# The last stores of an attention-and-feed-forward kernel, dealt anew to two DMA queues

## The chip, the cores and the metric

The kernel runs on one core of one Trainium2 chip. The metric is the device time of one execution in microseconds, as the median of several runs. All times below are microseconds, unless they are marked ns.

## What is computed

The first half is routing attention: queries and keys get a cluster by their nearest centroid, and a query sees only keys of its own cluster. The second half is a feed-forward block on the result. For this change only the end of the second half matters:

```python
scores = np.where(mask, scale * np.matmul(q, k.transpose(0, 1, 3, 2)), -1e9)
attn = softmax(scores)                      # rows
x = np.matmul(attn, v)                      # 4 batches, bridged to (3072, 512)
h = x @ w_in                                # (3072, 2048)
g = h * (1.0 / (1.0 + np.exp(-1.702 * h)))
out = g @ w_out                             # (3072, 512), float32
```

The output is 4 batches of 768 rows of 512 floats.

## The kernel before

`fast` does the whole work; `general` follows under a condition that these inputs don't meet, so every engine jumps over its code to the end of the program (line 34). After the attention, the feed-forward half runs batch by batch (`for b in range(B)`, B = 4). Each batch first makes the hidden values G with `first7`, then the output with seven calls of `second49`, one for each product in `ORDER = (1, 2, 3, 6, 5, 7, 4)` of a Strassen-like scheme. The output of a batch is held transposed in four quarters, Y[11], Y[12], Y[21] and Y[22]; each is 128 partitions by 2 (index m) by 384 (rows of the output). The quarters come complete in the order 11, 12, 22, 21.

`store(b, n, m, q, queues)` (line 940) brings quarter n, or a part of it, to the output. First VectorE transposes it in 32x32 blocks into another tile, one instruction (line 951) for each m. Then four DMAs (line 955), one for each group of 32 partitions, write it. `queues[r % len(queues)]` deals these four to the queues that are named: with `nc.sync` alone all go out on SyncE's queue (SPq in the profile), with `(nc.sync, nc.scalar)` they go out alternately on SyncE's and ScalarE's (ACTq). `q` selects halves of the rows, QT = 192 rows each. A whole quarter goes in DMAs of 32x12x64 floats (96 KB), half of its rows with both m in 32x6x64 (48 KB), half of its rows with one m in 32x6x32 (24 KB).

In the last batch the stores are placed in the last two calls of `second49` through `extra(at)`, which draws steps from generators. In the last call (k = 6, product 4) `tail()` is drawn. Its first step, at `extra(0)`, stores all of Y[22]. Its second step, at `extra(2)`, comes when all of Y[21] is complete except for the rows 0 to 191 of m = 1: these still lack the last product, which is added in line 928 (`add(c[:, 1, 0:QT], x, c[:, 1, 0:QT])`). After the loop over k, the last `store` brings these.

The order of instructions on each engine is the order in which they are recorded. Each DMA raises one of eight completion semaphores when it has landed, and it waits until the DMA that had this semaphore before has landed. The two queues share the eight semaphores. The built program shows which semaphore each DMA has: the third and fourth DMA of Y[22], on SPq, have numbers 4 and 5 and wait for the first and second DMA that ACTq issues for Y[21], which have the same numbers. The wait of a DMA for its data or its semaphore holds up everything behind it on the same queue.

Of the kernel before, what the change touches and what calls it, by code (L numbers as in the profile page):

```python
# [38 lines left out]
def fast(  # L39
# [26 lines left out]
    nc = tc.nc  # L66
# [4 lines left out]
    P = 128  # L71
# [12 lines left out]
    SQ = 32  # L84
# [520 lines left out]
    def sums_w(i):  # L605

        if i >= B * FB:
            return
        f = i % FB
        S = wq.tile([P, 3, 2, P], FP32, name="W")  # L610
        w_of[i] = {1: S[:, 0], 2: S[:, 1], 3: A_in(1, 0, f), 4: S[:, 2]}
        S = w_of[i]
        A11, A12, A22 = A_in(0, 0, f), A_in(0, 1, f), A_in(1, 1, f)
        if i < FB:
            sums(nc.gpsimd, ((S[3], A11, "-", S[3]),))
        sums(nc.gpsimd, ((S[2], A22, "-", S[3]), (S[1], S[2], "+", A11),
                         (S[4], A12, "-", S[2])))
# [122 lines left out]
    def sums_z(engine, f):  # L740
        sums(engine, ((Sz(3, f), Bz(0, 0, f), "-", Bz(0, 1, f)),
                      (Sz(2, f), Bz(1, 1, f), "-", Sz(3, f)),
                      (Sz(1, f), Sz(2, f), "+", Bz(0, 0, f)),
                      (Sz(4, f), Bz(1, 0, f), "-", Sz(2, f))))
# [16 lines left out]
    def turn_w(i):  # L761
        a = W_of(i)
        sums(nc.vector, ((a(0, 1), a(0, 0), "-", a(0, 1)),))

    def keep_w(k, o):

        a = W_of(ORDER[k])
        s2, s1, s4 = o
        for i, (o, x, op, z) in enumerate((
                (s2, a(1, 1), "-", a(0, 1)), (s1, s2, "+", a(0, 0)),  # L770
                (s4, a(1, 0), "-", s2))):
            sums(nc.gpsimd, ((o, x, op, z),))
            nc.sync.dma_start(out=kept_w[k, i], in_=o)

    def spare_y():
        return [Y[n].rearrange("p a t -> p (a t)")[:, 0:FQ * P].rearrange(
            "p (f n) -> p f n", n=P) for n in (12, 21, 22)]
# [3 lines left out]
    def load_sums(k, made=False):  # L781
        W[k] = ws.tile([P, 3, FQ, P], FP32, name="Wz")
        if made:
            keep_w(k, [W[k][:, i] for i in range(3)])
            return
        for i in range(3):
            nc.sync.dma_start(out=W[k][:, i], in_=kept_w[k, i])
# [50 lines left out]
    def first7(b, f, X, T):  # L838

        S = w_of.pop(b * FB + f)  # L840

        def product(a, x):
            ps = ps_b.tile([P, 512], FP32, name="b")
            for c in range(2):
                nc.tensor.matmul(out=ps[:, 0:HALF], lhsT=a[:, c], rhs=x(c),  # L845
                                 start=(c == 0), stop=(c == 1))
            return ps[:, 0:HALF]

        def finish(g):
            nc.scalar.activation(out=g, in_=g, func=AF.Gelu_apprx_sigmoid,  # L850
                                 scale=2.0)

        g1, g2 = G[:, f], G[:, f + FB]
        p = product(A_in(0, 0, f), lambda c: X[0, 0, c])
        nc.scalar.copy(g1[:, 0], p)
        p = product(S[2], lambda c: T[2, c])
        add(g2[:, 1], p, g1[:, 0])
        p = product(S[1], lambda c: T[1, c])
        add(g1[:, 1], p, g2[:, 1])
        p = product(S[3], lambda c: T[3, c])  # L860
        add(g2[:, 0], p, g2[:, 1])
        add(g2[:, 1], p, g1[:, 1])
        p = product(S[4], lambda c: X[1, 1, c])
        add(g1[:, 1], p, g1[:, 1])
        finish(g2[:, 1])
        p = product(A_in(1, 1, f), lambda c: T[4, c])
        add(g2[:, 0], p, g2[:, 0])
        finish(g1[:, 1])
        p = product(A_in(0, 1, f), lambda c: X[1, 0, c])
        add(g1[:, 0], p, g1[:, 0])  # L870
        finish(g2[:, 0])
        finish(g1[:, 0])

    def after7(f):

        sums(nc.vector, ((G[:, f, 1], G[:, f + FB, 1], "-", G[:, f, 1]),))
        if f >= FQ:
            for _ in sums_t(0, slice(f - FQ, f - FQ + 1)):
                pass
# [57 lines left out]
                    5: ((Y[12], y, "+", Y[12]), (Y[22], y, "+", Y[21])),  # L937
                    7: ((Y[22], y, "+", Y[22]), (Y[21], y, "+", Y[21]))}[i])

    def store(b, n, m=slice(0, 2), q=slice(0, 2), queues=(nc.sync,)):  # L940

        h, t = divmod(n, 10)
        h, t = h - 1, t - 1
        o = {11: T_of[4], 12: E[0], 22: E[1], 21: E[2]} if b < B - 1 else {
            11: T_of[4], 12: T_of[4], 22: T_of[2], 21: T_of[3]}
        o = o[n].rearrange("p a t -> p (a t)").rearrange(
            "p (j m i) -> p j m i", m=2, i=SQ)
        at, to = q.start * QT, q.stop * QT
        o = o[:, at // SQ:to // SQ]
        for one in range(m.start, m.stop):  # L950
            nc.vector.transpose(out=o[:, :, one], in_=Y[n][:, one, at:to])
        rows = out[b * S + t * HALF + at:b * S + t * HALF + to]
        for r in range(P // SQ):
            col = r * P + (2 * h + m.start) * SQ
            queues[r % len(queues)].dma_start(
                out=rows[:, col:col + (m.stop - m.start) * SQ].rearrange(
                    "(j t) i -> t j i", t=SQ),
                in_=o[r * SQ:(r + 1) * SQ, :, m].rearrange(
                    "t j m i -> t j (m i)"))
# [20 lines left out]
    def do(steps, n):  # L980
        for _ in range(n):
            next(steps, None)
# [3 lines left out]
    for b in range(B):  # L986
        for f in range(FB):
            first7(b, f, *XT)
            sums_w(b * FB + f + 2)
            if f:  # L990
                after7(f - 1)
            do(pend, 1)
            if b == 0 and f < 3:
                for n in range(3 * f, min(3 * f + 3, FB)):
                    sums_z((nc.gpsimd, nc.vector, nc.vector)[n % 3], n)
            if b == 0 and f in (3, 4):
                for i in ORDER[0:4] if f == 3 else ORDER[4:]:
                    turn_w(i)
            if b == 0 and f >= 3:
                for k in {3: (0,), 4: (1, 2), 5: (3,), 6: (4,), 7: ()}[f]:  # L1000
                    keep_w(k, spare_y())
                if 5 <= f < 7:
                    load_sums(f - 5)
        after7(FB - 1)
        if b < B - 1:
            for h in range(2):
                for hp in range(HP):
                    x = xT_of[b + 1, h, hp] = xp.tile([P, HALF], FP32,
                                                      name="x")
                    nc.sync.dma_start(out=x, in_=kept[b, h, hp])  # L1010
            made = sums_x(b + 1)
        else:
            made = iter(())

        def stores(b, *todo, **how):
            for n in todo:
                store(b, n, **how)
                yield

        both = dict(queues=(nc.sync, nc.scalar))  # L1020

        def tail():
            store(b, 22)
            yield
            store(b, 21, slice(0, 1), slice(0, 1), **both)
            store(b, 21, q=slice(1, 2), **both)
            yield

        def chain(*todo):
            for steps in todo:  # L1030
                yield from steps

        def sums_of_x():
            for XT[:] in made:
                yield

        x_steps = sums_of_x()
        final = b == B - 1

        for k in range(7):  # L1040
            nxt = sums_t(k + 1) if k < 6 else iter(())
            more = {1: sums_G(6), 2: sums_G(5), 3: sums_G(4),
                    4: stores(b, 11), 5: stores(b, 12) if final else x_steps,
                    6: tail() if final else x_steps}.get(k, iter(()))
            if b == B - 1 and k < 2:
                test(k)
            if (b, k) == (B - 1, 6):
                is_bad = nc.values_load(bad[0:1, 0:1], min_val=0, max_val=1)

            def extra(at):  # L1050
                do(nxt, (2, 1, 1)[at])
                do(more, ((1, 0, 1) if final else (0, 4, 4))[at] if k == 6
                   else (0, 0, 4)[at] if k == 2 else (0, 2, 2)[at])

            second49(k, extra, final)
            if k < 5:
                load_sums(k + 2, b == 0 and k > 2)
            elif b < B - 1:
                load_sums(k - 5)
        pend = () if final else stores(b, 12, 22, 21)  # L1060
        if final:
            store(b, 21, slice(1, 2), slice(0, 1), **both)
    return is_bad
@with_exitstack
def general(
# [436 lines left out]
```

## Time and profile before

| | us |
|---|---|
| median of 3 runs | 911.01 |
| lowest and highest | 910.65, 911.41 |
| the profiled execution, whole | 910.43 |
| span in its profile | 908.5 |
| TensorE busy | 888.4 |
| VectorE busy | 728.6 |
| GpSimd busy | 492.1 |
| ScalarE busy | 363.3 |

The profiled execution is 1.93 longer than its span: this part lies outside the recorded instructions. Positions in the profile, such as 897.36, are counted from the start of the span. A row of the timeline has start, length, engine, line, operation, output and input, and a count of instructions. A "q" after an engine (SPq, ACTq, DVEq, PEldq) marks its sequencer: issues of DMAs, waits and branches. The start of a DMA's row is the start of its issue, not of its transfer, and its length is that of the issue. TENSOR_TENSOR and STREAM_TRANSPOSE on DVE are VectorE's sums and transposes.

### The profile page before, as it was taken

The numbers are of one execution on the slowest core, as the hardware profiler recorded it, in microseconds if no ns is written. First come the engines' busy times: TensorE is split into PE (matmuls) and PEld (weight loads), VectorE is DVE, ScalarE is ACT, GpSimd is POOL, SyncE is SP. The second block draws the span as 40 slices with busy tenths as digits, with TensorE's granted clock in tenths as the row PEclk, the third lists the DMA queues.
The fourth block names the chain that finished last, engine by engine and source line by source line (L and its number), as shares of the span: only waits on it lengthen the run. The fifth ranks groups of instructions, "written<-read, shape, count | busy, mean of one in ns | idle before, by whom it ended". The sixth has DMA issues, their size and how long they took to land.

```text
span 908.5 us, 17741 instructions
## 1 busy us (share of the span) xinstructions
PE 888.4 (98%) x6712; PEld 577.7 (64%) x6712; DVE 728.6 (80%) x1170; ACT 363.3 (40%) x816; POOL 492.1 (54%) x469
## 2 busy tenths in 40 slices
PE   8999999999999999999999999999999999999994
PEld 3344444444444445557996557997557997557994
DVE  4999999998899997998998556797556797557894
ACT  3777767777676773322111222112222112222110
POOL 5899989998999998693274221243221243220220
PEclk9999999999999999999999999999999999999998
DMA  9465556666665210036213202322202322200323
GB/s 176 117 131 107 102 119 129 146 136 132 132 132 122 85 43 18 0 117 232 70 53 109 48 1 70 103 74 90 48 1 70 105 70 93 47 1 1 105 75 69
DMA packets 178397, 78.97 MB, mean 87 GB/s; under 512 B 155272, under 2 KB 161536, under 8 KB 178304
## 3 DMA queue, kind: packets, MB, share of 16 engines
q1 hardware_dynamic: 176912, 77.53, 35.4%
q8 instruction: 55, 0.90, 0.5%
q10 hardware_dynamic: 1392, 0.23, 0.2%
q14 instruction: 38, 0.31, 0.1%
HBM read 61.03 MB, written 16.70 MB: 86 GB/s over the span
## 4 chain that ended last, share of the span: by engine, by line
PE 81%; DVE 9%; DMA 3%; issue 2%; SPq 2%; ACT 2%; POOL 0%; DVEq 0%; ACTq 0%
PE b L845 32%; PE b L895 23%; PE s L467 11%; PE o L532 9%; PE m L549 3%; PE s L490 2%; DVE G L593 2%; DMA raw<-in_moe_w_out_dram 2%; DVE E L593 1%; ACT A L498 1%; SPq L418 1%; DVE Tx L593 1%; PE m L343 1%; DMA line<-row 1%; DVE x L570 1%
## 5 line engine op out<-in xcount | busy, mean ns | idle before, releaser
L516 POOL TENSOR_TENSOR sum<-sum,A 128x384 f32<-128x384 f32 x252 | 264.0, 1082 | 35.8 <-ACT A L498 22.6
L836 DVE TENSOR_TENSOR G<-b,G 128x384 f32<-128x384 f32 x224 | 123.0, 556 | 99.2 <-PE b L845 89.4
L498 ACT ACTIVATE A<-s 128x768 f32<-128x768 f32 x192 | 144.7, 803 | 93.9 <-PE s L490 73.8
L593 POOL TENSOR_TENSOR Y<-y,Y 128x768 f32<-128x768 f32 x28 | 67.4, 2422 | 175.0 <-DVE y L836 151.0
L467 PE MATMUL s<-T,T 64*64 64x384 f32 x1536 | 144.5, 491 | 2.7 <-ACT A L498 0.9
L850 ACT ACTIVATE G<-G 128x384 f32<-128x384 f32 x128 | 66.3, 523 | 198.9 <-DVE G L836 197.6
L532 PE MATMUL o<-A,inv 64*64 64x384 f32 x1536 | 141.3, 483 | 0.0
L593 POOL TENSOR_TENSOR W<-w_in 128x256 f32<-128x256 f32 x32 | 23.6, 736 | 164.2 <-PE b L845 163.8
L593 DVE TENSOR_TENSOR G<-G 128x768 f32<-128x768 f32 (+1 forms) x92 | 104.1, 1156 | 0.0
L467 PEld LDWEIGHTS s<-T,T 64*64 64x64 f32 x1536 | 52.0, 132 | 79.1 <-ACT A L498 52.0
L845 PE MATMUL b<-Tx,w_in 128*128 128x384 f32 x256 | 93.0, 486 | 0.0
L845 PE MATMUL b<-x,W 128*128 128x384 f32 x256 | 93.0, 486 | 0.0
L845 PE MATMUL b<-x,w_in 128*128 128x384 f32 x256 | 88.6, 486 | 0.0
L532 PEld LDWEIGHTS o<-A,inv 64*64 64x64 f32 x1536 | 58.7, 133 | 38.2 <-issue 33.3
L845 PEld LDWEIGHTS b<-x,W 128*128 128x128 f32 x256 | 48.6, 190 | 33.9
L845 PEld LDWEIGHTS b<-Tx,w_in 128*128 128x128 f32 x256 | 48.6, 190 | 33.9
L845 PEld LDWEIGHTS b<-x,w_in 128*128 128x128 f32 x256 | 48.5, 190 | 33.5 <-issue 0.6
L895 PE MATMUL b<-G,w_out 128*128 128x192 f32 x320 | 55.9, 326 | 0.0
L895 PEld LDWEIGHTS b<-G,w_out 128*128 128x128 f32 x320 | 52.7, 190 | 1.1
L895 PE MATMUL b<-E,Wz 128*128 128x192 f32 x288 | 51.5, 328 | 1.4 <-DVE E L593 1.4
L895 PEld LDWEIGHTS b<-E,Wz 128*128 128x128 f32 x288 | 47.1, 190 | 3.4 <-POOL Wz L593 1.3
L845 PE MATMUL b<-Tx,W 128*128 128x384 f32 x128 | 46.6, 487 | 1.5 <-DVE Tx L593 1.5
(169 smaller groups left out, 1357.5 us busy)
## 6 DMA issues: line engine op xcount, KB each, us to landing
Wz<-kept_w SPq DMA_DIRECT2D x78, 256.0 KB
raw<-in_moe_w_in_dram SPq DMA_DIRECT2D x16, 512.0 KB
raw<-in_moe_w_out_dram SPq DMA_DIRECT2D x16, 512.0 KB
inv<-in_v_dram SPq DMA_DIRECT2D x16, 384.0 KB
in<-in_q_dram SPq DMA_DIRECT2D x60, 96.0 KB
in<-in_k_dram SPq DMA_DIRECT2D x60, 96.0 KB
kept<-x SPq DMA_DIRECT2D x24, 192.0 KB
x<-kept SPq DMA_DIRECT2D x24, 192.0 KB
```

The costliest lines, as they stand in the source:

```text
L343: nc.tensor.matmul(out=ps[r:r + SQ, w * NJ * SQ:(w + 1) * NJ * SQ] .rearrange("p (j t) -> p j t", t=SQ), lhsT=cT[:, p % HP].rearrange("p a ...
L467: nc.tensor.matmul(out=ps[c:c + D, a, 0:HALF], lhsT=T[p, 1][rows, kt * P + c:kt * P + c + D], rhs=T[p, 0][rows, h * HALF:(h + 1) * HALF], ...
L490: nc.tensor.matmul(out=s_of[u][c:c + D, a, :], lhsT=rows_of[1, p % 2][rows, kt * P + c:kt * P + c + D], rhs=rows_of[0, p % 2][rows, h * HA ...
L498: nc.scalar.activation(out=A_of[u], in_=s_of.pop(u), func=AF.Exp, scale=SCALE)
L516: nc.gpsimd.tensor_tensor(out=sum_of[g][:, a], in0=(A_of[u - 1] if kt == 1 else sum_of[g])[:, a], in1=A_of[u][:, a], op=ALU.add)
L532: nc.tensor.matmul(out=o_of[g][a * D:(a + 1) * D, r, 0:HALF], lhsT=v_in[p][rows, a, kt, :], rhs=A[rows, a, :], start=(kt == 0), stop=(kt = ...
L549: nc.tensor.matmul(out=ps[a * D:(a + 1) * D, 0:HALF], lhsT=twos, rhs=sm[:, a, :], start=(i == 0), stop=(i == len(parts) - 1))
L593: engine.tensor_tensor(out=o, in0=a, in1=b, op=(ALU.add if op == "+" else ALU.subtract))
L836: nc.vector.tensor_tensor(out=o, in0=p, in1=a, op=ALU.add)
L845: nc.tensor.matmul(out=ps[:, 0:HALF], lhsT=a[:, c], rhs=x(c), start=(c == 0), stop=(c == 1))
L850: nc.scalar.activation(out=g, in_=g, func=AF.Gelu_apprx_sigmoid, scale=2.0)
L895: nc.tensor.matmul(out=ps, lhsT=A[n][:, f], rhs=M[n][:, f], start=start and f == 0, stop=(f == FQ - 1), skip_group_check=True)
```

## The change

Four parts, all in the last batch:

1. `store` gets a parameter `turned`, which says which m are transposed in this call, apart from `m`, which says which go out. With `queues=()` it only transposes.
2. In the second step of `tail()`, the rows 192 to 383 of Y[21], both m, are transposed and stored first, in four DMAs of 48 KB, all on SyncE's queue. Before, they were stored on both queues.
3. After that, m = 0 of the rows 0 to 191 is only transposed. Before, it was transposed first and stored in four DMAs of 24 KB on both queues.
4. After the loop, m = 1 of the rows 0 to 191 is transposed, and both m go out in four DMAs of 48 KB on both queues. Before, m = 1 alone went out in four DMAs of 24 KB.

Y[22] is stored by the same call as before.

```diff
-    def store(b, n, m=slice(0, 2), q=slice(0, 2), queues=(nc.sync,)):
+    def store(b, n, m=slice(0, 2), q=slice(0, 2), queues=(nc.sync,),
+              turned=slice(0, 2)):
...
-        for one in range(m.start, m.stop):
+        for one in range(turned.start, turned.stop):
             nc.vector.transpose(out=o[:, :, one], in_=Y[n][:, one, at:to])
         rows = out[b * S + t * HALF + at:b * S + t * HALF + to]
-        for r in range(P // SQ):
+        for r in range(P // SQ if queues else 0):
...
-        both = dict(queues=(nc.sync, nc.scalar))
-
         def tail():
             store(b, 22)
             yield
-            store(b, 21, slice(0, 1), slice(0, 1), **both)
-            store(b, 21, q=slice(1, 2), **both)
+            store(b, 21, q=slice(1, 2))
+            store(b, 21, q=slice(0, 1), queues=(), turned=slice(0, 1))
             yield
...
         if final:
-            store(b, 21, slice(1, 2), slice(0, 1), **both)
+            store(b, 21, q=slice(0, 1), turned=slice(1, 2),
+                  queues=(nc.sync, nc.scalar))
```

## The prediction

> **What bounds the kernel now.** I read the page first, then the chain of waits near the end, then the timeline of the two queues that issue stores, then SyncE's own waits, the branch at line 34, and the DMA traffic.
>
> ```profile
> span 908.5 us, 17741 instructions
> ...
> q8 instruction: 55, 0.90, 0.5%
> ...
> q14 instruction: 38, 0.31, 0.1%
> ...
> PE 81%; DVE 9%; DMA 3%; issue 2%; SPq 2%; ACT 2%; POOL 0%; DVEq 0%; ACTq 0%
> ```
>
> TensorE bounds the kernel as a whole (81% of the chain), but the change doesn't touch its work. The chain of waits from 895 on shows where arithmetic ends:
>
> ```profile
> 894.86 0.18 PE b L895
> ...
> 897.36 0.38 DVE Tx L951
> ```
>
> The last transpose ends at 897.74, 10.8 before the end of the span. These 10.8 are stores and the way out, and only they can change. The issues in them, each from a narrow window of the timeline:
>
> ```profile
> 887.94 1.91 SPq L955 DMA_DIRECT2D out_dram<-Tx  x4
> 891.99 0.83 SPq L955 DMA_DIRECT2D out_dram<-Tx  x2
> 898.14 1.85 SPq L955 DMA_DIRECT2D out_dram<-Tx  x2
> 896.59 0.85 ACTq L955 DMA_DIRECT2D out_dram<-Tx  x2
> 897.54 0.40 ACTq L955 DMA_DIRECT2D out_dram<-Tx  x1
> 898.52 1.46 ACTq L955 DMA_DIRECT2D out_dram<-Tx  x1
> 900.82 0.97 SPq L955 DMA_DIRECT2D out_dram<-Tx  x2
> 901.89 1.92 SPq L955 DMA_DIRECT2D out_dram<-Tx  x4
> ```
>
> Y[22] is ready at 891.96, and two of its four stores are issued at 891.99. The other two go out only at 898.14. They wait for completion semaphores 4 and 5, which ACTq's first two stores of Y[21] hold; these are issued at 896.59 and land just before 898.14. Its fourth issue takes 1.39 of the 1.85. Then SyncE waits 0.8 more for ACTq's third store (semaphore 6), until 900.8, and issues six stores of Y[21] in 0.97 + 1.92 with small gaps, until 903.82. SyncE's waits say the same:
>
> ```profile
> SPq L955 <- DMA out_dram<-Tx: 6.1, 2, 5.3
> SPq L34 <- SPq L34: 2.7, 1, 2.7
> ```
>
> The 5.3 is 892.82 to 898.14. The 2.7 is the branch at line 34:
>
> ```profile
> L34 SPq EVENT_SEMAPHORE  x8: 17/17/17, 906.6 to 907.2; - x8
> ...
> L34 ACTq COMPARE_BRANCH  x1: 54/54/54, 900.5 to 900.5; - x1
> L34 ACTq EVENT_SEMAPHORE  x1: 17/17/17, 903.3 to 903.3; - x1
> L34 SPq COMPARE_BRANCH  x1: 45/45/45, 903.9 to 903.9; - x1
> ```
>
> From branch to next instruction VectorE takes 2.8 (897.44 to 900.27), ScalarE 2.8 and SyncE 2.7: a fixed price. SyncE's last store landed at 905.34 by the trace's semaphore records, 1.3 before SyncE went on at 906.6. So the end is set by **SyncE's last issue**: 903.82, plus 2.8 to 906.6, plus 1.9 of closing steps to 908.5.
>
> **What the Trainium skill says.** Its page "DMA: Bandwidth & Descriptors", section "Why a DMA increments its semaphore by 16 and not by 1", says that each of up to 16 DMA engines adds one when its share has landed, so that only the full count means landed. The trace agrees, and shows stragglers: ACTq's third store had 15 of its 16 counts by 899.78, and the last one at 900.76. The page "Runtime: NRT & Kernel Launch", section "Instruction fetch mechanics", says that code comes by DMA in blocks of 16 KiB and that a taken branch must fetch its target. The trace has such fetches on the queues q8 and q14:
>
> ```profile
> DMA packets 595, 0.17 MB, mean 120 GB/s; under 512 B 593, under 2 KB 593, under 8 KB 593
> ...
> q8 instruction: 1, 0.02, 5.9%
> q14 instruction: 1, 0.01, 2.4%
> ```
>
> That is the window 898.2 to 899.6. The one packet on q8 has 16 KB and lasts from 898.26 to 899.57; the packet records show no store's packet from the engine that it sits on until 899.56. This makes the straggler. It comes 0.6 after TensorE's instruction at line 34 (897.67), so it belongs to TensorE, which the change leaves alone. The DMA page's section "Issuing engines are not separate DMA queues" says that both queues end up on the same 16 engines; the straggler, which a fetch imposes on a store of ACTq and through it on SPq, agrees.
>
> **The change, part by part.**
>
> *Y[22] (same call, other semaphores).* In the changed program its four stores have semaphores 6, 7, 0 and 1. Their last users are loads of line 787 and stores of Y[12], all landed by 890.6. So all four issue at 891.99, in the 1.91 that Y[12]'s four took: until 893.9. The 5.3 wait and the 1.85 of issue at 898.14 go. SyncE is free long before the next data.
>
> *Rows 192 to 383 of Y[21], SPq alone.* Their two transposes come first now, ready at 896.83 (two of the three in the 896.19 row, 0.89). The four 48 KB stores have semaphores 2, 3, 4 and 5. Numbers 2 and 3 are free: two issues from 896.84 to about 897.7. Numbers 4 and 5 are what ACTq's two stores use, and in the program's order those come first. So **the wait is not removed but moved**: the third store of this half waits until ACTq's first store has landed. Behind it on SPq stand one more store of this half, both last stores of SPq, the branch and the end.
>
> *VectorE.* Four transposes and one sum as before, in another order: nothing. The last transpose still ends at 897.74, since TensorE's part was ready at 896.33 already. If the order cost something it would be one transpose, 0.34.
>
> *Number of DMAs.* Before, twelve for Y[21], six on each queue; now eight, six of them on SPq and two on ACTq. SPq has six as before, but two are issued early, so four stand behind the wait instead of six.
>
> *ACTq.* It now waits for the last transpose (897.75), then issues its first store until 898.1 (0.35 as in the 896.59 row) and its second until 898.6. When do they land? The nearest row is ACTq's third store of before: same size, issued until 897.93, and landed at 900.76. The new first store is 0.2 later, but what held the old one was the fetch until 899.57, which stays, so I take 900.7, and 0.2 more for the second, as before (900.76 and 900.96). Bounds: 900.1, if the share on the blocked engine lands half a microsecond after the fetch; 901.1, if ScalarE's own fetch, which comes earlier with its branch (about 1.0 after it, from 900.56 to 898.7), catches the rest.
>
> *Sum.* SyncE goes on at 900.7 + 0.05 and issues four stores. The last four of before took 1.92, with the same two kinds of small waits: done at 902.67. Before it was 903.82: 1.15 less, with the bounds between 1.75 and 0.75. The last landing is hidden: issue end plus 1.5 (905.34 - 903.82) is 904.2, and SyncE leaves the branch at 902.67 + 2.8 = 905.4. If that cover were gone, the excess would be added. ACTq is ready at 898.6 + 2.8 = 901.4, early. So the span goes from 908.5 to 907.35, the profiled execution from 910.43 to 909.28, and the median, which is 0.58 above it, from 911.01 to **909.8**.
>
> **The rivals.**
>
> *A, faster by over 0.2%.* ACTq's stores land as its first two of before did, at most 1.4 after the wait for data ended (896.83 to 898.14): at 899.15 and 899.6. Then SyncE issues the third at once, the fourth at 899.65, and is done at 899.65 + 0.45 + 1.0 = 901.1, which is 2.7 less: 908.3. For it: less other traffic, as SPq has no 96 KB stores in flight at 898 to 900 any more. Against it: every 48 KB store here uses all 16 engines, and TensorE's fetch occupies one from 898.26 on, before the new packets can start.
>
> *B, slower.* The fetches of TensorE (until 899.57) and of ScalarE, now about 899.7 to 900.5, meet ACTq's landing one after the other, on one engine. Place: SPq's third store of Y[21]. Price: landing at 901.5 (ACTq's last store of before landed at 902.79, 0.8 after a packet of q14 that ended at 901.99), and one of the four issues blocked as in the 898.52 row, 1.46 instead of 0.45: done at 901.7 + 1.92 + 1.0 = 904.6, 0.8 more, 911.8. It decides when ACTq's first store lands after 901.85. For it: two issues of before were blocked in that way. Against it: they were blocked while three stores of ACTq and 192 KB of SPq queued at the occupied engine; now two of ACTq do.
>
> *C, no effect.* The end is set by the landing of the last stores and not by the issue: then 911.0. It needs a landing 1.3 later after its issue than before. Against it: less traffic at the end.
>
> **How the numbers follow.** The likeliest case, 0.66, gives 909.8 (909.2 to 910.3 by its bounds); A 0.22; C 0.07; B 0.05. About 0.2%, 1.8, is what a measurement of this kernel can tell from no change. The likeliest case and C lie within it, save a small part of the first; B mostly exceeds 911.0 by less than that. So faster 0.24, same 0.72, slower 0.04. The range 908.6 to 910.9 leaves out the lower part of A and all of B.
>
> **What would show it.** Y[22]'s four stores in one row at 891.99; a wait of SPq on a DMA at line 956 of about 3, from 897.7 to 900.7, in place of the 5.3 and 0.8 of before; SPq's branch near 902.7 and the first EVENT_SEMAPHORE after it 2.7 later. If that wait ends near 899.2, A holds. If it ends after 901.8, or an issue behind it takes over 1, B holds. If the gap behind SPq's branch grows, C holds. The prediction is wrong altogether if SPq's last issue no longer sets the end.

## The result and the profile after

| | before | after |
|---|---|---|
| median of 22 runs each | 910.62 | 909.46 |
| lowest and highest | 909.79, 911.42 | 908.60, 911.41 |
| ratio after to before, 95% interval | | 0.9987 (0.9981 to 0.9993) |
| span of the profiled execution | 908.5 | 907.1 |

The change makes the kernel 1.2 faster, 0.13%. That is less than the 0.2% taken above as what can be told from no change; with 22 runs of each, though, the interval lies wholly below 1.

The page and the chain of waits of the changed kernel, in which the transposes of `store` stand in line 952 and its DMAs in line 956:

```profile
span 907.1 us, 17734 instructions
...
PE 81%; DVE 9%; DMA 3%; issue 2%; SPq 2%; ACT 2%; POOL 0%; ACTq 0%; DVEq 0%
```

```profile
897.01 0.38 DVE Tx L952
```

The last transpose ends at 897.39, 0.34 earlier than in the profile of before. The difference is there before the changed stores begin: the first issue of Y[22] is 0.35 earlier too (891.64 and 891.99), and so is TensorE's branch (893.8 and 894.1). So positions are counted below from the end of the last transpose where kernels are compared. The timeline of the two issuing queues, each row from a narrow window:

```profile
891.64 1.89 SPq L956 DMA_DIRECT2D out_dram<-Tx  x4
896.51 0.80 SPq L956 DMA_DIRECT2D out_dram<-Tx  x2
897.43 0.85 ACTq L956 DMA_DIRECT2D out_dram<-Tx  x2
900.52 0.32 SPq L956 DMA_DIRECT2D out_dram<-Tx  x1
900.88 0.58 SPq L956 DMA_DIRECT2D out_dram<-Tx  x1
901.56 0.98 SPq L956 DMA_DIRECT2D out_dram<-Tx  x2
```

All of Y[22] goes out in one row at 891.64. Then SyncE issues two stores of Y[21], stands still, and issues its last four from 900.52 to 902.54. SyncE's waits and the branch:

```profile
SPq L956 <- DMA out_dram<-Tx: 3.2, 1, 3.2
SPq L34 <- SPq L34: 2.5, 1, 2.5
```

```profile
L34 SPq EVENT_SEMAPHORE  x8: 17/17/17, 905.2 to 905.7; - x8
...
L34 SPq COMPARE_BRANCH  x1: 45/45/45, 902.6 to 902.6; - x1
```

The 5.3 wait of before, which held half of Y[22], is replaced by a 3.2 wait in the middle of Y[21]. From the end of the last transpose to the end of SyncE's last issue it is 903.82 - 897.73 = 6.09 before and 902.54 - 897.39 = 5.15 after: 0.94 of the 1.43 by which the two spans differ. The earlier end of the arithmetic is 0.34 more, and a branch that is shorter by 0.15 is the rest.

### The profile page after: what moved, and what is told of

It reads as the page before. It is cut to its first block, busy times and chain, and to the rows that moved or that the text cites. A ratio compares the mean times of both kernels' runs of the same rounds, so it can differ in the third digit from the quotient of the medians.

```text
span 907.1 us, 17734 instructions
## 1 busy us (share of the span) xinstructions
PE 887.9 (98%) x6712; PEld 578.1 (64%) x6712; DVE 728.6 (80%) x1170; ACT 363.4 (40%) x816; POOL 492.3 (54%) x469
## 4 chain that ended last, share of the span: by engine, by line
PE 81%; DVE 9%; DMA 3%; issue 2%; SPq 2%; ACT 2%; POOL 0%; ACTq 0%; DVEq 0%
PE b L845 32%; PE b L895 23%; PE s L467 11%; PE o L532 9%; PE m L549 3%; PE s L490 2%; DVE G L593 2%; DVE E L593 1%; ACT A L498 1%; DMA raw<-in_moe_w_out_dram 1%; SPq L418 1%; DVE Tx L593 1%; PE m L343 1%; DMA raw<-in_moe_w_in_dram 1%; DMA line<-row 1%
```

## The experiments

Theory: the end is set by SyncE's last issue; SyncE is held by a wait for ScalarE's landing, on a completion semaphore that both queues use in turn; the landing is late because one DMA engine is busy with TensorE's code. Rivals: the gain belongs to taking the half off ScalarE's queue; the last landing sets the end; the store lands late for another reason.

All seven at a glance. Each ratio is from 5 (e4) to 21 runs (e5 and e7), beside runs of before on the same chip; e1 to e4 ran on one chip, e5 to e7 on another. The last two columns come from the profile: from the end of the last transpose to the end of SyncE's last issue, and from there to the end of the span.

| kernel | ratio to before (95%) | to last issue | from there to the end |
|---|---|---|---|
| before | | 6.09 | 4.7 |
| changed | 0.9987 (0.9981 to 0.9993) | 5.15 | 4.6 |
| e1, merged half alone | 0.9977 (0.9967 to 0.9987) | 4.36 | 4.6 |
| e2, SyncE half alone | 1.0003 (0.9995 to 1.0011) | 6.82 | 4.7 |
| e3, SyncE for all | 0.9981 (0.9969 to 0.9994) | 4.22 | 4.6 |
| e4, Y[22] on GpSimd's queue | 0.9957 (0.9944 to 0.9971) | 0.91 | 5.4 |
| e5, changed again | 0.9983 (0.9976 to 0.9990) | 5.13 | 4.5 |
| e6, two stores less | 0.9977 (0.9967 to 0.9986) | 3.74 | 4.7 |
| e7, leaving later | 0.9982 (0.9975 to 0.9988) | 4.82 | 4.8 |

### e1: the merged transfers without the move to SyncE

```diff
-            store(b, 21, q=slice(1, 2))
+            store(b, 21, q=slice(1, 2), queues=(nc.sync, nc.scalar))
```

> The last quarter's last row half in four whole transfers, as in the changed kernel, but the half before it stays on both queues. Theory (the end is set by SyncE's last issue, and SyncE is held by waits for ScalarE's landings): ScalarE issues four stores, SyncE four. SyncE's first store of Y[21] waits for ScalarE's first, to about 898.2, its third waits for ScalarE's third, the one that TensorE's code fetch delays, to about 900.6; two issues follow, so the last is done near 901.5 instead of 902.5, the span near 906.0, about 1.0 below the changed kernel and 2.2 below before (ratio to before near 0.9976). Rival (the gain came from taking the next-to-last half off ScalarE's queue): no gain without it, ratio near 1.000.

Measured: 0.9977, last issue 4.36 after the last transpose. SyncE's timeline and waits in this kernel:

```profile
897.66 3.50 SPq L956 DMA_DIRECT2D out_dram<-Tx  x4
```

```profile
SPq L956 <- DMA out_dram<-Tx: 6.8, 3, 5.0
SPq L34 <- SPq L34: 2.6, 1, 2.6
```

SyncE has four stores of Y[21] instead of six, three of them with a wait for ScalarE's landing, the last such wait until 900.31. The sum over waits (6.8) is longer than in the changed kernel (3.2), and the kernel is faster all the same, since only two issues stand behind the last wait instead of four. The rival falls: the gain belongs to the merged transfers. Taking the next-to-last half off ScalarE's queue costs about 0.8 of it in the profile (5.15 against 4.36); that rests on one profile of each, as the intervals of the two ratios overlap.

### e2: the move to SyncE without the merged transfers

```diff
-            store(b, 21, q=slice(0, 1), queues=(), turned=slice(0, 1))
+            store(b, 21, slice(0, 1), slice(0, 1), (nc.sync, nc.scalar),
+                  slice(0, 1))
...
-            store(b, 21, q=slice(0, 1), turned=slice(1, 2),
-                  queues=(nc.sync, nc.scalar))
+            store(b, 21, slice(1, 2), slice(0, 1), (nc.sync, nc.scalar),
+                  slice(1, 2))
```

> The half before the last on SyncE alone, as in the changed kernel, but the last row half in eight small transfers over both queues, as before. Theory: Y[22] goes out early as in the changed kernel, but SyncE's four stores of the next-to-last half wait for ScalarE's four, of which the later ones land near 900.6, and four small ones stand behind: about five to six issues after 900.6, last one done near 903.2, span near 907.8, 0.3 to 0.8 below before (ratio 0.9991 to 0.9997). Rival (this part is the gain): ratio 0.9987 or less.

Measured: 1.0003, no gain; in the profile SyncE's last issue is even 0.7 later than before. I had expected a small gain. ScalarE's last small store, SyncE's waits, and what SyncE does after them:

```profile
898.81 2.01 ACTq L956 DMA_DIRECT2D out_dram<-Tx  x1
```

```profile
SPq L956 <- DMA out_dram<-Tx: 7.4, 2, 5.1
```

```profile
901.60 3.28 SPq L956 DMA_DIRECT2D out_dram<-Tx  x7
```

Four stores of SyncE need the landings of ScalarE's four in turn, and two of them wait long. The second of these waits ends with ScalarE's second store, which landed at 901.58, 1.18 after the end of TensorE's code fetch (900.40). That is 3.5 after the last transpose, where 3.2 was expected. All seven issues that were left stand behind it, and not five or six. Y[22] goes out early here too, and it brings nothing: the wait has only moved. This part of the change alone is worth nothing.

ScalarE's last issue was blocked for 2.01, until 0.42 after the fetch had ended. That looks like the culprit and isn't: its store landed at 902.57, and SyncE was ready for it at 902.44, so SyncE lost about 0.1 by it.

### e3: no second queue, no wait between queues

```diff
-            store(b, 21, q=slice(0, 1), turned=slice(1, 2),
-                  queues=(nc.sync, nc.scalar))
+            store(b, 21, q=slice(0, 1), turned=slice(1, 2))
```

> All eight stores of Y[21] on SyncE's queue, none on ScalarE's, so that no store waits for one of the other queue. Theory: the waits vanish; four issues from 896.5 and four from 897.4, some of them blocked until about 900 by TensorE's code fetch; last issue done between 900.2 and 900.9 instead of 902.5, span near 905.1, ratio to before near 0.9965. Rival A (a second queue is needed to keep the rate of issues up): last issue later than in the changed kernel, ratio above 0.9987. Rival C (the landing of the same bytes sets the end): span as in the changed kernel, 907.1, ratio 0.9987.

Measured: 0.9981, where 0.9965 was expected. The waits of SyncE and its eight stores:

```profile
SPq L956 <- DVE Tx L952: 4.7, 2, 3.5
SPq L34 <- SPq L34: 2.6, 1, 2.6
```

```profile
896.00 5.11 SPq L956 DMA_DIRECT2D out_dram<-Tx  x8
```

No wait for a landing is left, as the theory says; with it 0.9 goes (5.15 to 4.22). But eight issues take 5.11, not the 3.6 of eight by 0.45. Four of them last 0.75, 0.77, 0.81 and 0.77, the others 0.32 to 0.46. Each of the four overlaps a packet on q8 or q14 and ends 0.13 to 0.38 after that packet has ended. I had counted only TensorE's fetch as a cause of such blocking. But three of the four end just after a packet of 8 KB on q14, and these come at the times of VectorE's and ScalarE's ways out.

### e4: Y[22] out of the way

```diff
-            store(b, 22)
+            store(b, 22, queues=(nc.gpsimd,))
...
-            store(b, 21, q=slice(1, 2))
+            store(b, 21, q=slice(1, 2), queues=(nc.sync, nc.scalar))
```

GpSimd is idle here, and its DMAs have semaphores of their own; the eight stores of Y[21] then wait for none that is in flight.

> Y[22] on GpSimd's queue, and Y[21] in eight transfers over SyncE's and ScalarE's queues, so that no semaphore is shared by stores in flight. Theory: no wait but for data; both queues issue two from 896.5 and two from 897.4 and are done near 898.4; both come out of the branch at 901.1; what lands last is the share behind TensorE's code fetch, near 900.9, so the span is near 903.0 to 903.5, ratio to before near 0.994. Rival C (landing sets the end already in the changed kernel): no better than 0.9987. Rival (GpSimd's stores are slow enough to become the end): ratio above 0.9965.

Measured: 0.9957, about 3.9 below before. The kernel differs from e1 in the queue of Y[22] alone. SyncE's timeline and the way out:

```profile
896.55 1.80 SPq L956 DMA_DIRECT2D out_dram<-Tx  x4
```

```profile
L34 SPq EVENT_SEMAPHORE  x8: 17/17/17, 901.6 to 902.2; - x8
...
L34 SPq COMPARE_BRANCH  x1: 45/45/45, 898.4 to 898.4; - x1
```

SyncE waits only for data and is done 0.9 after the last transpose. Now its first step after the branch comes 3.1 later and not 2.6. It starts 0.02 after ScalarE's last store has landed (901.58 by the semaphore records), and that store raises the semaphore for which this step waits, so that landing seems to set the end here, as in no other kernel. That isn't settled: ScalarE, which waits for no landing at line 34, needed 3.3 too, and the code fetches of the engines lie close together here. The gain is smaller than the 5.5 that the expected ratio 0.994 stands for; the span, 903.7, is 0.2 above the top of the expected range. This version has the lowest ratio of all.

### e5 and e6: what stands behind the wait

e5 is the changed kernel again. e6 leaves out SyncE's last two stores:

```diff
-        for r in range(P // SQ if queues else 0):
+        for r in range(P // SQ if queues else 0) if groups is None else groups:
...
-                  queues=(nc.sync, nc.scalar))
+                  queues=(nc.sync, nc.scalar), groups=(1, 3))
```

> The changed kernel itself, beside the next two on the same chip. Ratio to before near 0.9987, SyncE's last issue about 5.1 after the last transpose has ended (6.1 before the change).

> The changed kernel without SyncE's last two stores: two of the four groups of 32 columns of the last quarter's first 192 rows are not written. ScalarE's stores, and with them the wait, stay. Theory (SyncE's last issue sets the end): 0.39 and 0.55 of issue and the small gaps go, so the span is 1.0 to 1.1 below the changed kernel, ratio to before near 0.9976. Rival C (the last landing sets the end): the store that is then last lands near 903.2 in the changed kernel's count, before SyncE would come out of the branch at 904.1, so the span falls by less than 0.5.

Measured: e5 0.9983, e6 0.9977; the intervals overlap, so what follows rests on the profiles. In e6 SyncE's last two issues, and its way out:

```profile
899.79 0.80 SPq L956 DMA_DIRECT2D out_dram<-Tx  x2
```

```profile
L34 SPq EVENT_SEMAPHORE  x8: 17/17/17, 903.4 to 903.9; - x8
...
L34 SPq COMPARE_BRANCH  x1: 45/45/45, 900.6 to 900.6; - x1
```

The last issue comes 1.39 earlier than in e5, counted from the last transpose: 1.1 as expected, 0.3 from a wait that happened to be shorter. The span follows by 1.2 (8.47 after the last transpose instead of 9.68), though the last landing comes only 0.7 earlier (5.69 after the last transpose instead of 6.43). It is the issue and not the landing that sets the end. The other kernels, e4 apart, say the same: from SyncE's last issue to the end it is 4.5 to 4.8 in all of them (the table's last column), while from the last landing, by the semaphore records, it is anything from 2.8 to 3.5.

### e7: the code fetches moved

```diff
             store(b, 21, q=slice(0, 1), turned=slice(1, 2),
                   queues=(nc.sync, nc.scalar))
+            for i in range(3):
+                sums(nc.vector, ((E[0], E[0], "+", E[0]),))
+                if i == 1:
+                    ps = ps_b.tile([P, 512], FP32, name="b")
+                    nc.tensor.matmul(out=ps[:, 0:SQ], lhsT=ident,
+                                     rhs=E[0][:, 0, 0:SQ], start=True,
+                                     stop=True)
```

> The changed kernel with three sums on VectorE after the last transpose (each near 0.95) and one matmul on TensorE that waits for the second: both engines come to the branch at line 34 about 2 later, and their code fetches too. Stores, queues and semaphores are as in the changed kernel. Theory (the wait of SyncE is for the share of ScalarE's store behind TensorE's fetch): ScalarE's first store lands 1.6 to 1.7 after the last transpose instead of 3.1, its second 0.5 later; SyncE's last issue comes 3.5 to 4.0 after the last transpose instead of 5.1, and the span falls by 1.1 to 1.6 (ratio to before near 0.9972), though the kernel has more work. Rival (the store lands late for another reason, such as the traffic of the two queues, or the write itself): the wait ends as before, and the ratio stays at 0.9987 or rises by the added work.

Measured: 0.9982, beside 0.9983 of e5. The timeline of SyncE's last four issues, its waits, and the DMA traffic from 898.9 to 900.6:

```profile
897.80 0.32 SPq L956 DMA_DIRECT2D out_dram<-Tx  x1
898.29 0.38 SPq L956 DMA_DIRECT2D out_dram<-Tx  x1
898.77 0.39 SPq L956 DMA_DIRECT2D out_dram<-Tx  x1
899.20 1.71 SPq L956 DMA_DIRECT2D out_dram<-Tx  x1
```

```profile
SPq L34 <- SPq L34: 2.8, 1, 2.8
SPq L956 <- DMA out_dram<-Tx: 1.9, 2, 1.8
```

```profile
q8 instruction: 1, 0.02, 5.6%
q14 instruction: 2, 0.02, 3.3%
```

The last transpose ends at 896.09. ScalarE's first store landed 1.69 after it, where it was 3.2 in e5, and the second 0.5 later: exactly as expected, though stores, queues and semaphores are the same. That shows that the long wait was for a share behind a code fetch.

e7 moves VectorE's fetches as well as TensorE's. Which of them held the store is told by the trace of the changed kernel, here from 898 to 899.4:

```profile
q8 instruction: 1, 0.02, 4.9%
q14 instruction: 1, 0.01, 1.4%
```

The 16 KB packet on q8, TensorE's, lasts from 898.25 to 899.34. ScalarE's two stores are 384 packets of data. Of these 360 began before 899.34 and the last 24, one sixteenth, from 899.34 on. The semaphore of the first store had 14 of its 16 counts by 899.13 and the 15th at 899.76, which is 1.08 after the end of the 8 KB packet on q14 (898.68). The last came at 900.51, 1.17 after TensorE's packet. So two counts came late, each a little over 1 after a fetch had ended, and the one that ended the wait is the one behind TensorE's.

But the time stays nearly as it was. TensorE's way out has two packets of 16 KB, one during its branch and one 0.6 after its next instruction. In the changed kernel, with the branch from 893.80 to 897.55, the first packet lies at 895.15 to 896.03, before the last transpose has ended, and the second is the one that held the store. In e7, with the branch from 897.97 to 901.92, the second comes at 902.59, when SyncE has issued everything. These are the windows 894 to 897 of the changed kernel and 902 to 904.5 of e7:

```profile
q8 instruction: 1, 0.02, 1.8%
```

```profile
q8 instruction: 1, 0.02, 2.7%
```

The first packet lies at 898.97 to 900.49 in e7, and SyncE's last issue meets it: 1.71, done 0.42 after the packet. What left the wait came back in the issue: 4.82 to the last issue instead of 5.13, where 3.5 to 4.0 was expected. So e7 shows what the wait was for, by the landing; it doesn't show in the time what the kernel would gain without the fetch.

## Why the prediction was right

**The forecast.** 909.8 from a median of 911.01, a step of 1.2; measured 909.46 from 910.62, a step of 1.2. The interval of the ratio, 0.9981 to 0.9993, is a step of 0.6 to 1.7, all of it within the 1.8 that the prediction took for "same". That the two steps agree to 0.1 is in part luck. In the profiles the last issue came 0.94 sooner after the last transpose, where 1.15 was predicted, and the changed kernel measured again beside e6 and e7 gained 1.3 by the medians.

**What sets the end.** SyncE's last issue, plus a fixed way out. Shown: the way out is 4.5 to 4.8 in eight profiles, with the last issue between 3.7 and 6.8 after the last transpose; e6 moves the end by leaving out issues, and by more than it moves the last landing. Rival C falls for this change, and may hold in e4, where the issues end early.

**Y[22].** Four issues in one row, 1.89, where 1.91 was predicted. That this is worth nothing by itself can be read from before: the fourth issue of Y[22] ended there at 900.00, and SyncE then still waited 0.8 for ScalarE's third store. e2, which has it too and is no faster, agrees.

**The moved wait.** Predicted to end at 900.7, 3.0 after the last transpose, by analogy with a store of before; it ended 3.1 after it. That TensorE's fetch is the reason, which the prediction argued from the packets, is shown by e7 and the packets of the changed kernel together: the last sixteenth of the data starts when the fetch ends, and with the fetches moved, the same store lands at 1.7. Rival A, which had the store land like the first two of before, is what e7 makes true of the landing. Its price of 1.4 was misread, though: 896.83 to 898.14 is 1.31, and the store began at 896.59 and landed at 898.12, which is 1.53.

**Four issues instead of six.** Predicted 1.92, measured 2.02 (900.52 to 902.54): one issue took 0.58. Rival B, blocked issues, didn't decide the changed kernel, but its mechanism is real: it makes SyncE's last issue 1.71 long in e7 and costs about 1.3 in all in e3 (four long issues of 3.09, less four of 0.44). In e2 it makes an issue of ScalarE 2.01 long and costs hardly anything, since SyncE wasn't waiting for that store. The prediction gave blocked issues 0.05 and tied them to a late landing; e3 and e7 have them without one.

**What the prediction didn't price.** It took the parts together. Apart, they are worth different things: merging the last half's small transfers alone gives 0.9977, the move of the next-to-last half to SyncE alone 1.0003, which is nothing. In the changed kernel the move puts two more issues behind the wait and, by the profiles, gives back about 0.8 of what the merging gains.

**Sums that don't come out.** 911.01 less 1.15 is 909.86, not 909.8. The range 908.6 to 910.9 leaves out C's 911.0 as well, and of A also the figure 908.3 itself. Neither changes the argument.

**Left open.** Why the arithmetic ends up to 2.0 earlier or later from profile to profile (896.1 to 898.1) wasn't tried. It wasn't tried either to separate a block of the issue by one engine's fetch from that by another's, or why some issues that meet a fetch aren't blocked.

## What to carry to other kernels

When stores of two queues share completion semaphores, look up in the built program which store waits for which: a store that is ready can stand behind one that isn't, and moving a transfer to the other queue may merely move that wait. At the end of a kernel, count the issues behind the last such wait, rather than the bytes. Here fewer and larger transfers gained (0.9977 in e1), and whether they went out on two queues or on one (0.9981 in e3) made no difference that can be told. Best was a third queue with its own semaphores for what is ready early: from e1 to e4 that alone took the last issue from 4.4 to 0.9 after the arithmetic.

## What the runs showed of the hardware that was not expected

From 880 on, the 164 issues on SyncE's and ScalarE's queues that overlap no code fetch in time take 0.32 to 0.49 in the nine profiles. Of the 37 that overlap one, 14 take longer, 0.55 to 2.01. Of these 14, 13 end at nearly the same time after a packet: 0.13 to 0.22 after one of 8 KB on q14 (issues of 0.55 to 0.89) and 0.38 to 0.44 after one of 16 KB on q8 (issues of 0.56 to 2.01). The other is one of 0.61 in before, which ended 0.29 after an 8 KB packet, beside a second one. The remaining 23 are not longer: in e2 an issue of 0.32 lies wholly within a 16 KB packet. What decides it isn't known.

The first store to land after the end of TensorE's second 16 KB packet landed 1.15 to 1.19 after that end in seven kernels: before, changed, e1, e2, e3, e5 and e6. In e4 it was the third store to land that came 1.15 after it. In e7 the first store to land after the earlier of the two packets came 1.10 after that one.

The prediction takes from the page "Runtime: NRT & Kernel Launch" of the Trainium skill, section "Instruction fetch mechanics", that code comes in blocks of 16 KiB and that a taken branch must fetch its target. The page says the latter of a target that lies outside the pages already held. The packets on q14 have 8 KB (38 of them make 0.31 MB in before), so the 16 KiB hold here for q8 alone.

The way from the branch to the next instruction was 2.5 to 2.8 for SyncE and for ScalarE in all kernels but e4 (3.1 and 3.3), and 2.8 to 3.3 for VectorE. TensorE's branch itself lasted 3.5 to 4.0 (3465 ns before, 3745 after, 3965 in e4).
